# A spectral mixer with a gated token MLP: two pairs of the way back share a visit of TensorE

## The chip, the core and the metric

The kernel runs on one core of a Trainium2 chip. The metric is the device time of one execution in microseconds. Three runs of the kernel before took 365.48, 365.69 and 365.95 us; the median is 365.69 us.

## What is computed

x has 2048 tokens of 512 channels, all in fp32.

```python
xn = layernorm(x)                                   # over the channels
s  = irfft2(rfft2(xn) * (w_r + 1j * w_i))           # 2-D FFT over tokens and channels, filtered, and back
u  = gelu(einsum("bsd,sf->bdf", xn, w1) + b1)       # MLP over the tokens: 2048 -> 1792
y  = einsum("bdf,fs->bds", u, w2) + b2              # 1792 -> 2048
out = x + s * silu(transpose(y))
```

## The kernel before

The first 200 us or so make the layer norm, the way there of the transform, the filter, and the hidden layer `u`. The change touches only what follows: the second matrix product and the way back of the transform, in the loop over `p` (lines 1038 to 1099).

**Pairs and products.** The 2048 output tokens are 16 blocks of 128 rows. Blocks `p` and `p + 8` are a pair; there are eight. Each pair's output (2 blocks by 512 channels) is a 2 by 2 product of blocks, made with seven products in place of eight (a Strassen form). Their order is `ORDER = (1, 2, 5, 6, 3, 7, 4)`; the place of a product in it, 0 to 6, is called its slot `k`. A product is 21 matmuls of 128x128 weights by 256 columns (seven hidden tiles, each in three parts of a high and a low split), all into one half bank of PSUM. Products 1, 6, 7 and 4 go to `bx` (bank 3 for even pairs, bank 2 for odd ones), 2 to `by` (bank 4), 5 and 3 to `bz` (bank 5), each in the left half. Products 1, 2 and 5 start an accumulation; 6, 7, 4 and 3 add to what is there, so the state in between has to be read first: `p1`, `p5`, `v2` are copies by ScalarE, and `c11`, `c12`, `c22` are sums that VectorE reads out of PSUM. `c22 = bx + p5` is read after product 7 and before product 4.

**Forms.** The weights of a product are a "form" of w2: a high part that ScalarE makes (line 820) and a low part that VectorE makes (line 824), in three rotating buffers `w2f`. In slot `k` the form for the product three slots later is made, in the buffer that the product of slot `k` has just read. After product 7 VectorE also makes sums of blocks for the next pair (`sums_of_blocks`, two operations of 128x896). The w2 blocks come by DMA from SyncE; two sums of blocks per pair are made by a second, accumulating DMA from GpSimd, which waits for the first one to land.

**The way back.** For each pair, four gathers copy the pair's filtered rows out of `ey` into `yt` (two on ScalarE, then two on VectorE). TensorE then has three small parts, which are called a visit here: E (`even_channels`, 16 matmuls of a 64x64 quarter of the array, fp32, each recorded twice), O (`odd_channels`, four of 128x128), both from `yt` into banks 6 and 7, and S (`spectral`, four 64x64 matmuls by 512 columns, from `y` into banks 0 and 1). Between the channel parts (E, O) and the token part (S) stands `unfolded`, a generator of three pieces: a copy by ScalarE and five VectorE operations into `es`; a sum into `y`; a difference into `y`. `finish` multiplies S's result by the gate (`Silu`, ScalarE) into `r`, and four DMAs of GpSimd's queue add `r` to the output in memory, which holds x already; two of them belong to each block.

**Where it stands.** `SLOTS` gives for each pair the slot after which the visit stands, and a plan: after which slots a gather ("g") or a piece of `unfolded` ("s") is made. `PARTS` gives the order of E, S and O in the visit. In pair 0, E stands after slot 5 and O after slot 6; in pairs 1 to 6 the visit ESO stands after slot 5, with the S of the pair before; in pair 7 SEO after slot 3, and its own S after slot 5. So in pairs 0 to 7 something of the way back stands between products 7 and 4.

**What sets the order.** From line 937 on, every engine's instructions are kept in the order of the program (`Kept`), so each engine has one fixed queue. Waits come from the data: a tile's new use waits for the readers of its old one, and PSUM is followed by bank.

**Buffers.** The pool `fin` holds `es`, `y` and `yt` with one buffer each, `r` with two (one for each block of a pair), `c` with two and the gates `g` with four.

Of the kernel before, what the change touches and what calls it, by code (L numbers as in the profile page):

```python
# [9 lines left out]
F32 = mybir.dt.float32  # L10
F32R = mybir.dt.float32r
AF = mybir.ActivationFunctionType
# [3 lines left out]
P = 128  # L16
# [18 lines left out]
WT = 3  # L35


SLOTS = ((6, {3: "gggg", 6: "s"}), (5, {0: "s", 1: "sgg", 2: "gg", 5: "s", 6: "s"}),
         (5, {0: "s", 1: "gg", 2: "gg", 5: "s", 6: "s"}),
         (3, {0: "s", 1: "gg", 2: "gg", 3: "s", 4: "ss"}))  # L40

PARTS = ("O", *["ESO"] * 6, "SEO")

KD = np.concatenate([np.arange(0, 256, 4), np.arange(2, 256, 4), np.arange(1, 256, 2)])

# [94 lines left out]
def spectral_mixer_kernel(tc, x, w1, b1, w2, b2, wk, we, wx, c_f, c_ft, c_d, c_i, c_g, c_h, out):  # L142
# [19 lines left out]
    with tc.tile_pool(name="ps", bufs=1, space=PSUM) as psp, ExitStack() as left, ExitStack() as right:  # L162
# [778 lines left out]
        def new_sums(p):  # L941
            return (fp.tile([P, 2, 2, 2, P], F32, name=f"es{p}", tag="es"),
                    fp.tile([P, 2, 2, 2, P], F32, name=f"y{p}", tag="y"))

        def new_gates(p):
            return [fp.tile([P, D], F32, name=f"g{j}", tag="g", bufs=4) for j in (p, p + NP)]


        first_sums, gates = new_sums(0), {0: new_gates(0)}
# [3 lines left out]
        def gathered(p):  # L953


            yt = fp.tile([P, 2, 4, 2, 64], F32, name=f"yt{p}", tag="yt")
            yts[p] = yt
            for i, j in enumerate((p, p + NP)):
                for h in range(2):
                    to = yt[:, i, :, h ^ i].rearrange("p b (s c) -> p b s c", c=2)  # L960
                    yield V.tensor_copy(to, ey[:, :, h::2, j]) if i else A.activation(to, ey[:, :, h::2, j], AF.Copy)

        def tokens_of(yt, i, b):
            return yt[:, i, b].rearrange("p e c -> p (e c)")

        def even_channels(p):


            for i in range(2):
                for s in range(2):  # L970
                    at = slice(128 * i + 64 * s, 128 * i + 64 * s + 64)
                    for e in range(2):
                        for r, rows in enumerate((slice(0, 64), slice(64, P))):
                            T.matmul(ps[64 * e:64 * e + 64, 6 + r, at], yts[p][rows, i, 2 * s, e], ci[rows, 2 * s, :64],
                                     start=True, stop=True)

        def odd_channels(p):

            for i in range(2):
                for s in (1, 0):  # L980
                    at = 256 + 128 * s
                    T.matmul(ps[:, 6 + i, at:at + P], tokens_of(yts[p], i, 2 * s + 1), ci[:, 2 * s + 1], start=True, stop=True)

        def unfolded(p):

            es, y = new_sums(p) if p else first_sums
            e0, e1 = (es[:, :, k].rearrange("p i b c -> p i (b c)") for k in range(2))
            first, odd = ps[:, 6, :256].rearrange("p (i s c) -> p i s c", s=2, c=64), ps[:, 6:8, 256:]
            other = y.rearrange("p i h q c -> p (i h q c)")[:, :257]
            A.activation(other, ps[:, 7, :257], AF.Copy)  # L990
# [12 lines left out]
            ys[p] = y.rearrange("p i h q c -> p i (h q c)")  # L1003
            yield

        def spectral(p):

            y = ys.pop(p)
            for e, cols in enumerate((slice(0, 64), slice(64, P))):
                for r, rows in enumerate((slice(0, 64), slice(64, P))):  # L1010
                    i = e ^ r
                    T.matmul(ps[cols, i], cft[rows, cols], y[rows, i], start=True, stop=True)

        def gate(g, j, cols, src, scale):
            A.activation(g[:, cols], src, AF.Silu, bias=b2t[:, j:j + 1], scale=scale)
# [5 lines left out]

        def finish(g, j, cols):
            r = last_rows[:, j // NP] if last_rows is not None else fp.tile([P, D], F32, name=f"r{j}", tag="r", bufs=2)
            for to, a, b in zip(mirrored(r[:, cols], True), mirrored(ps[:, j // NP, cols], False), mirrored(g[:, cols], False)):
                V.tensor_mul(to, a, b)
            if last_rows is not None:
                for part in quarter_rows if cols is left_ else (cols,):
                    V.tensor_add(r[:, part], r[:, part], xr[j // NP][:, part])
            for queue, (rows, tokens) in zip((SY, SY if cols is right_ else A), halved):
                if last_rows is None:  # L1030
                    G.dma_start(out[tokens, j, cols], r[rows, cols], accum_op=ALU.add)
                else:
                    queue.dma_start(out[tokens, j, cols], r[rows, cols])
# [4 lines left out]
        for p in range(NP):  # L1038
            j0, j1 = p, p + NP
            more = p + 1 < NP  # L1040
            if p:
                gates[p] = new_gates(p)
            g0, g1 = gates[p]
            bx, by, bz = banks(p)
            slot, plan = SLOTS[min(p, 2) + (not more)]
            gathering = gathered(p)
            for k, n in enumerate(ORDER):
                started = not p and k < 2
                if not started:
                    products(p, n)  # L1050
                if n == 1 and p:
                    p1 = copied(f"p1_{p}", bx, w2p)
                elif n == 5:
                    p5 = copied(f"p5_{p}", bz, fp)
                elif n == 6:
                    v2 = copied(f"v2_{p}", bx, fp)
                elif n == 7:
                    c22 = summed(f"c22_{p}", bx, p5)
                if n == 3 and more:
                    c12 = summed(f"c12_{p}", bz, v2)  # L1060
                if not started:
                    ready.extend(w for w in [next(wforms, None)] if w is not None)
                if n == 2:
                    c11 = summed(f"c11_{p}", by, p1)
                elif n == 6:
                    gate(g0, j0, left_, c11, 1.0)
                elif n == 3 and more:
                    gate(g0, j0, right_, c12, 1.0)
                elif n == 7:
                    gate(g1, j1, right_, c22, -1.0)  # L1070
                elif n == 4:
                    for cols in (left_,) if more else quarter_rows:
                        gate(g1, j1, cols, bx[:, cols], -1.0)
                if not p and k == slot - 1:
                    even_channels(p)
                if k == slot:
                    for part in PARTS[p]:
                        {"S": spectral, "E": even_channels, "O": odd_channels}[part](p - (part == "S"))
                    yts.pop(p)
                    pieces = unfolded(p)  # L1080
                    if p:
                        for g, j in zip(gates.pop(p - 1), (j0 - 1, j1 - 1)):
                            finish(g, j, whole)
                for what in plan.get(k, ""):
                    next(gathering if what == "g" else pieces)
                if n == 3 and not more:
                    gate(g0, j0, right_, summed(f"c12_{p}", bz, v2), 1.0)
                if more and n == 7:
                    sums_of_blocks()
                if not more and k == 2:  # L1090
                    xr = [where.tile([P, NH * P], F32, name=f"xr{i}", tag="s1", bufs=1)[:, :D] for i, where in enumerate((w2p, fp))]
                    for to, j in zip(xr, (j0, j1)):
                        for rows, tokens in halved:
                            SY.dma_start(to[rows], x[tokens, j])
# [43 lines left out]
```

## Time and profile before

| | |
|---|---|
| median of three runs | 365.69 us |
| the profiled execution | 365.77 us |
| its span | 364.0 us |
| TensorE busy (share of the span) | 358.1 us (98%) |
| VectorE busy | 307.8 us (85%) |
| ScalarE busy | 211.2 us (58%) |
| GpSimd busy | 87.2 us (24%) |
| granted TensorE clock in the stage of the pairs | 1.00 |
| pair 2, 241.6 to 261.4 us: TensorE, VectorE, ScalarE busy | 19.80, 15.73, 10.66 us |

The span is the time from the first to the last instruction that the profiler recorded; the execution's own time is 1.77 us longer. In rows of the timeline the first number is the start in us from the span's start, the second the length of the row; rows of one kind that follow each other are merged, with their count at the end. The end of a matmul is modelled, so the start of the next row is the better measure of how long a group took. The bracket at the end of a row names idle time of the engine and what ended it. PE is TensorE, PEld its weight loads, DVE VectorE, ACT ScalarE, POOL GpSimd.

### The profile page before, as it was taken

What the parts mean: (1) busy time and instruction counts of PE and PEld (TensorE: products, weight loads), DVE (VectorE), ACT (ScalarE), POOL (GpSimd) and SP (SyncE); (2) the same over time, 40 slices, a digit from 0 to 9 for tenths busy, and PEclk for the clock granted to TensorE, in tenths of its full rate; (3) what the DMA queues carried; (4) which work ended last, traced back from release to release, by engine and by line L of the source; (5) the groups of instructions that cost most, each with busy time, mean ns of one, the idle gap of its engine ahead of it and who ended that gap; (6) DMA issues with size and microseconds to landing.
All of it is one profiled execution on the core that took longest, in us unless ns stands there. A gap on an engine that the chain in (4) does not pass through costs nothing.

```text
span 364.0 us, 8851 instructions
## 1 busy us (share of the span) xinstructions
PE 358.1 (98%) x3476; PEld 310.8 (85%) x3476; DVE 307.8 (85%) x590; ACT 211.2 (58%) x385; POOL 87.2 (24%) x134
## 2 busy tenths in 40 slices
PE   8999999999999999999999999999999999999994
PEld 7788888888877778777888999989898989898993
DVE  5899999967699997999995988687887878797974
ACT  4877778867634426755237884655464546565431
POOL 4233333323222012220120001040503132130330
PEclk9999999999999999999999999999999999999999
DMA  7977999306695687996577288698888989898624
GB/s 207 246 190 187 231 288 333 133 0 155 172 275 181 189 241 193 252 239 201 174 236 156 101 236 172 180 185 200 189 184 212 178 224 164 240 162 209 114 27 90
DMA packets 33293, 68.66 MB, mean 189 GB/s; under 512 B 4612, under 2 KB 19380, under 8 KB 33124
## 3 DMA queue, kind: packets, MB, share of 16 engines
q1 hardware_dynamic: 24276, 42.44, 42.2%
q0 software_dynamic: 8496, 25.01, 32.0%
q10 hardware_dynamic: 480, 0.66, 0.6%
q8 instruction: 27, 0.44, 0.6%
q14 instruction: 14, 0.11, 0.1%
HBM read 59.70 MB, written 8.13 MB: 186 GB/s over the span
## 4 chain that ended last, share of the span: by engine, by line
PE 96%; DVE 1%; DMA 1%; issue 0%; ACT 0%; DVEq 0%
PE ps L139 96%; DMA x<-in_x_dram 1%; DVE stm L244 0%; DVE rows L139 0%; DVE h L469 0%; DVE w1l L469 0%; DVE h L272 0%; ACT g L139 0%; DVE v2m L221 0%; DVE mvm L220 0%; DVE tm L229 0%; ACT sdm L223 0%; DVEq L1134 0%; DVE r0m L228 0%; DVE nbm L237 0%
## 5 line engine op out<-in xcount | busy, mean ns | idle before, releaser
L139 PE MATMUL ps<-h,w1h 128*128 128x512 f32 x400 | 116.3, 397 | 0.1
L139 PEld LDWEIGHTS ps<-h,w1h 128*128 128x128 f32 x400 | 72.9, 188 | 19.9 <-issue 4.9
L139 PE MATMUL ps<-h,w1l 128*128 128x512 f32 x200 | 67.6, 390 | 0.0
L139 DVE TENSOR_TENSOR w2f<-a,w2f 128x896 fp32r<-128x896 f32 x36 | 39.2, 1090 | 16.4 <-ACT w2f L139 16.4
L139 ACT ACTIVATE w2f<-a 128x896 fp32r<-128x896 f32 x36 | 37.2, 1033 | 20.0 <-PE ps L139 7.6
L139 PEld LDWEIGHTS ps<-h,w1l 128*128 128x128 f32 x200 | 37.5, 188 | 8.1
L139 PE MATMUL ps<-fb,w2f 128*128 128x256 f32 x336 | 42.1, 280 | 0.0
L139 POOL DMA_DIRECT2D s<-in_w_dram x14 | 18.3, 1311 | 96.8 <-DMA s<-in_w_dram 71.7
L139 PE MATMUL ps<-fa,w2f 128*128 128x256 f32 x336 | 41.4, 278 | 0.0
L139 PEld LDWEIGHTS ps<-fb,w2f 128*128 128x128 f32 x336 | 39.9, 188 | 0.9 <-DVE c L139 0.8
L139 PE MATMUL ps<-fc,w2f 128*128 128x256 f32 x336 | 39.9, 277 | 0.0
L139 PEld LDWEIGHTS ps<-fa,w2f 128*128 128x128 f32 x336 | 39.9, 188 | 0.0
L139 PEld LDWEIGHTS ps<-fc,w2f 128*128 128x128 f32 x336 | 39.2, 188 | 0.0
L155 ACT ACTIVATE w1h<-w1s 128x512 fp32r<-128x512 f32 x26 | 16.2, 632 | 25.6 <-PE ps L139 10.8
L139 POOL DMA_DIRECT2D out_dram<-r x28 | 23.6, 1276 | 27.9 <-DVE r L139 27.9
L667 POOL DMA_DIRECT2D xc<-xc x16 | 9.8, 619 | 69.2 <-ACT xc L665 54.0
L308 POOL TENSOR_TENSOR ey<-t 128x256 f32<-128x256 f32 x16 | 15.7, 979 | 44.0 <-DVE t L306 44.0
L139 ACT ACTIVATE w2f<-s 128x896 fp32r<-128x896 f32 x15 | 15.3, 1022 | 14.2 <-PE ps L139 12.4
L139 DVE TENSOR_TENSOR w2f<-s,w2f 128x896 fp32r<-128x896 f32 x15 | 16.3, 1088 | 6.5 <-ACT w2f L139 6.4
L469 DVE TENSOR_TENSOR w1l<-w1r,w1h 128x384 fp32r<-128x384 f32 x32 | 21.3, 669 | 0.0
L139 PE MATMUL ps<-fd,w2f 128*128 128x256 f32 x168 | 20.7, 278 | 0.0
L268 ACT ACTIVATE h<-x,nbm,rsm 128x256 f32<-128x256 f32 (+1 forms) x34 | 18.4, 593 | 3.9 <-DVE nbm L263 3.1
(132 smaller groups left out, 602.3 us busy)
## 6 DMA issues: line engine op xcount, KB each, us to landing
a<-in_w_dram SPq DMA_DIRECT2D x22, 448.0 KB, 4.0
wt<-in_wk_dram POOLq DMA_DIRECT2D x16, 512.0 KB, 5.8
s<-in_w_dram SPq DMA_DIRECT2D x16, 448.0 KB, 4.1
s<-in_w_dram POOLq DMA_DIRECT2D x16, 448.0 KB, 6.5
w1s<-in_w_dram SPq DMA_DIRECT2D x52, 128.0 KB, 5.5
w1r<-in_w_dram SPq DMA_DIRECT2D x28, 192.0 KB, 5.1
xc<-xc POOLq DMA_DIRECT2D x16, 256.0 KB, 3.1
out_dram<-in_x_dram SPq DMA_DIRECT2D x4, 960.0 KB, 6.5
```

Source lines behind the costliest of these rows:

```text
L139: return lambda *args, **kw: self.keep(operation(*args, **kw))
L155: return A.activation(hi, src, AF.Copy), V.tensor_sub(lo, src, hi.bitcast(F32))
L268: keep(A.activation(to, v, AF.Identity, bias=m["nb"][:, i], scale=m["rs"][:, i, 1:2]))
L308: G.tensor_add(ey[:, 0::3, :, j], a, b)
L469: keep(V.tensor_sub(dst, src, hi.bitcast(F32)))
L667: keep(G.dma_start(*(v.rearrange("p s t c -> p s (t c)") for v in (there[c::2], here[1 - c::2, ::-1]))))
```

## The change

- Pair 0 has no visit; its gathers stay after slot 3. They go to two tiles of tag `r`, and so do those of pair 2.
- Pair 1's visit stands after slot 3 and holds E of pairs 0 and 1 and O of pairs 0 and 1. Pair 1's go to banks 0 and 1 (`transformed_to`). The gathers of pair 1 stand one slot earlier, after slots 0 and 1. `unfolded` of pair 0 stands after slots 3 and 4, that of pair 1 after slots 5, 6 and slot 0 of pair 2.
- Pair 2's visit stands after slot 4 and holds E of pair 2, S of pairs 0 and 1, and O of pair 2. S of pair 0 goes to bank 2 and, in two halves, to the right halves of banks 4 and 5 (`spectral_places`): six matmuls instead of four. `finish` of pair 0 stands after slot 4, with four multiplies of 128x128 in place of two of 128x256 for its second block; that of pair 1 after slot 5.
- `unfolded` of pair 2 stands after slot 6 and slot 0 of pair 3. From pair 3's visit on, all is as before.
- Tiles of the first pairs take other places: pair 0's `y` and pair 2's `es` that of `yt`, one gate of pair 2 that of `es`.

The diff, without changes of form alone:

```diff
-SLOTS = ((6, {3: "gggg", 6: "s"}), (5, {0: "s", 1: "sgg", 2: "gg", 5: "s", 6: "s"}),
-         (5, {0: "s", 1: "gg", 2: "gg", 5: "s", 6: "s"}),
-         (3, {0: "s", 1: "gg", 2: "gg", 3: "s", 4: "ss"}))
-PARTS = ("O", *["ESO"] * 6, "SEO")
+SLOTS = ((7, {3: "gggg"}), (3, {0: "gg", 1: "gg", 3: "s", 4: "ss", 5: "s", 6: "s"}),
+         (4, {0: "s", 1: "gg", 2: "gg", 6: "s"}), (5, {0: "ss", 1: "gg", 2: "gg", 5: "s", 6: "s"}),
+         (5, {0: "s", 1: "gg", 2: "gg", 5: "s", 6: "s"}), (3, {0: "s", 1: "gg", 2: "gg", 3: "s", 4: "ss"}))
...
+        def new_gate(j):
+            return fp.tile([P, D], F32, name=f"g{j}", tag="g", bufs=4)
+
         def new_gates(p):
-            return [fp.tile([P, D], F32, name=f"g{j}", tag="g", bufs=4) for j in (p, p + NP)]
+            if p == 2:
+                return [fp.tile([P, 2, D], F32, name="g2", tag="es")[:, 0], None]
+            return [new_gate(j) for j in (p, p + NP)]
...
-            yt = fp.tile([P, 2, 4, 2, 64], F32, name=f"yt{p}", tag="yt")
+            if p in (0, 2):
+                yt = [fp.tile([P, D], F32, name=f"yt{p}_{i}", tag="r", bufs=2) for i in range(2)]
+                yt = [t.rearrange("p (b h c) -> p b h c", b=4, h=2) for t in yt]
+            else:
+                yt = fp.tile([P, 2, 4, 2, 64], F32, name=f"yt{p}", tag="yt")
+                yt = [yt[:, i] for i in range(2)]
...
+        def transformed_to(p):
+            return 0 if p == 1 else 6
...
+        def unfolded_to(p):
+            if p > 2:
+                return new_sums(p)
+            es = first_sums[0] if p == 0 else fp.tile([P, 2, 2, 2, P], F32, name=f"es{p}", tag=("es", "yt")[p - 1])
+            y = first_sums[1] if p == 1 else fp.tile([P, 2, 2, 2, P], F32, name=f"y{p}", tag=("yt", "y")[p // 2])
+            return es, y
...
+        def spectral_places(p):
+            if p:
+                return [[(whole, ps[:, i])] for i in range(2)]
+            return [(whole, ps[:, 2])], [(left_, ps[:, 4, HD:]), (right_, ps[:, 5, HD:])]
+
         def spectral(p):
-            y = ys.pop(p)
+            y, places = ys.pop(p), spectral_places(p)
             for e, cols in enumerate((slice(0, 64), slice(64, P))):
                 for r, rows in enumerate((slice(0, 64), slice(64, P))):
                     i = e ^ r
-                    T.matmul(ps[cols, i], cft[rows, cols], y[rows, i], start=True, stop=True)
+                    for part, to in places[i]:
+                        T.matmul(to[cols], cft[rows, cols], y[rows, i, part], start=True, stop=True)
...
-            for to, a, b in zip(mirrored(r[:, cols], True), mirrored(ps[:, j // NP, cols], False), mirrored(g[:, cols], False)):
-                V.tensor_mul(to, a, b)
+            for part, src in spectral_places(j % NP)[j // NP] if cols is whole else [(cols, ps[:, j // NP, cols])]:
+                for to, a, b in zip(mirrored(r[:, part], True), mirrored(src, False), mirrored(g[:, part], False)):
+                    V.tensor_mul(to, a, b)
...
-            slot, plan = SLOTS[min(p, 2) + (not more)]
+            slot, plan = SLOTS[min(p, 4) + (not more)]
...
-                if not p and k == slot - 1:
-                    even_channels(p)
                 if k == slot:
-                    for part in PARTS[p]:
-                        {"S": spectral, "E": even_channels, "O": odd_channels}[part](p - (part == "S"))
-                    yts.pop(p)
-                    pieces = unfolded(p)
-                    if p:
-                        for g, j in zip(gates.pop(p - 1), (j0 - 1, j1 - 1)):
+                    done = (0, 1) if p == 1 else (p,)
+                    back = (0, 1) if p == 2 else (p - 1,) if p > 2 else ()
+                    for at in done[:1] if back else done:
+                        even_channels(at)
+                    for at in back:
+                        spectral(at)
+                    for at in done:
+                        odd_channels(at)
+                        yts.pop(at)
+                    pieces = chain(*map(unfolded, done))
+                    if back:
+                        for g, j in zip(gates.pop(back[0]), (back[0], back[0] + NP)):
                             finish(g, j, whole)
+                if p == 2 and k == slot + 1:
+                    for g, j in zip(gates.pop(1), (1, 1 + NP)):
+                        finish(g, j, whole)
```

More of the change, by code (lines that the diff above doesn't have):

```diff
@@ L959, in gathered @@
                 for h in range(2):
-                    to = yt[:, i, :, h ^ i].rearrange("p b (s c) -> p b s c", c=2)
+                    to = yt[i][:, :, h ^ i].rearrange("p b (s c) -> p b s c", c=2)
                     yield V.tensor_copy(to, ey[:, :, h::2, j]) if i else A.activation(to, ey[:, :, h::2, j], AF.Copy)
         def tokens_of(yt, i, b):
-            return yt[:, i, b].rearrange("p e c -> p (e c)")
+            return yt[i][:, b].rearrange("p e c -> p (e c)")
+        def transformed_to(p):
+            return 0 if p == 1 else 6
         def even_channels(p):
+            bank = transformed_to(p)
             for i in range(2):
@@ L973, in even_channels @@
                         for r, rows in enumerate((slice(0, 64), slice(64, P))):
-                            T.matmul(ps[64 * e:64 * e + 64, 6 + r, at], yts[p][rows, i, 2 * s, e], ci[rows, 2 * s, :64],
+                            T.matmul(ps[64 * e:64 * e + 64, bank + r, at], yts[p][i][rows, 2 * s, e], ci[rows, 2 * s, :64],
                                      start=True, stop=True)
@@ L981, in odd_channels @@
                     at = 256 + 128 * s
-                    T.matmul(ps[:, 6 + i, at:at + P], tokens_of(yts[p], i, 2 * s + 1), ci[:, 2 * s + 1], start=True, stop=True)
+                    T.matmul(ps[:, transformed_to(p) + i, at:at + P], tokens_of(yts[p], i, 2 * s + 1), ci[:, 2 * s + 1], start=True, stop=True)
+        def unfolded_to(p):
[4 more added lines that the diff above has]
+            return es, y
         def unfolded(p):
-            es, y = new_sums(p) if p else first_sums
+            es, y = unfolded_to(p)
+            bank = transformed_to(p)
             e0, e1 = (es[:, :, k].rearrange("p i b c -> p i (b c)") for k in range(2))
-            first, odd = ps[:, 6, :256].rearrange("p (i s c) -> p i s c", s=2, c=64), ps[:, 6:8, 256:]
+            first, odd = ps[:, bank, :256].rearrange("p (i s c) -> p i s c", s=2, c=64), ps[:, bank:bank + 2, 256:]
             other = y.rearrange("p i h q c -> p (i h q c)")[:, :257]
-            A.activation(other, ps[:, 7, :257], AF.Copy)
+            A.activation(other, ps[:, bank + 1, :257], AF.Copy)
             other = other[:, :256].rearrange("p (i s c) -> p i s c", s=2, c=64)
@@ L1069, in spectral_mixer_kernel @@
                 elif n == 7:
+                    if g1 is None:
+                        g1 = gates[p][1] = new_gate(j1)
                     gate(g1, j1, right_, c22, -1.0)
```

## The prediction

> **What bounds the kernel now.** I read the page first, then TensorE's timeline of the last stage, the waits, and the timelines of VectorE, ScalarE and GpSimd around one visit.
>
> ```profile
> span 364.0 us, 8851 instructions
> ...
> PE 96%; DVE 1%; DMA 1%; issue 0%; ACT 0%; DVEq 0%
> ```
>
> The profiled execution took 365.77 us, 1.77 more than its span; the median of the runs shown is 365.69. The chain that ended last is TensorE for 96% of the span, so in the last stage whatever lengthens TensorE's stream lengthens the kernel. That stream is, for each pair, seven products of 21 matmuls (numbers 1, 2, 5, 6, 3, 7, 4, in slots 0 to 6) and a visit of the way back: E (even channels), O (odd channels), S (token transform). Pair 0 first, then pair 1:
>
> ```profile
> 212.65 2.64 PE L139 MATMUL ps<-fa,w2f 128*128 128x256 f32 x21
> 215.13 2.63 PE L139 MATMUL ps<-fb,w2f 128*128 128x256 f32 x21
> 217.69 0.69 PE L139 MATMUL ps<-cd,yt 64*64 64x64 f32 x32
> 218.31 2.74 PE L139 MATMUL ps<-fb,w2f 128*128 128x256 f32 x21
> 220.89 1.05 PE L139 MATMUL ps<-cd,yt 128*128 128x128 f32 x8
> 221.70 2.72 PE L139 MATMUL ps<-fd,w2f 128*128 128x256 f32 x21
> ```
>
> ```profile
> 234.15 2.63 PE L139 MATMUL ps<-fb,w2f 128*128 128x256 f32 x21
> 236.72 0.69 PE L139 MATMUL ps<-cd,yt 64*64 64x64 f32 x32
> 237.23 1.04 PE L139 MATMUL ps<-y,cft 64*64 64x512 f32 x8
> 238.20 1.16 PE L139 MATMUL ps<-cd,yt 128*128 128x128 f32 x8
> 239.12 2.72 PE L139 MATMUL ps<-fb,w2f 128*128 128x256 f32 x21
> ```
>
> A product takes 2.47 us from start to start (212.65 to 215.13). A visit costs its own rows, 0.10 at its entry (234.15 + 2.47 = 236.62, E at 236.72) and 0.09 in the product behind it (2.72 against 2.63). In pair 1 E takes 0.51, S 0.97 and O 0.92.
>
> **What the visits hide.** Products 7 and 4 stand next to each other and add into the same bank; between them VectorE must read the bank (`c22`). Everywhere else a whole product lies between a product and the one that adds to its result.
>
> ```profile
> PEld ps L139 <- DVE c L139: 0.8, 1, 0.8
> ```
>
> ```profile
> 217.80 0.42 DVE L139 TENSOR_TENSOR c<-ps,p 128x256 f32<-128x256 f32 x1
> ```
>
> Pair 0 shows the wait: product 7 ends at 217.76 (215.13 + 2.63), `c22` runs from 217.80 to 218.22, product 4 starts at 218.31, 0.09 later. Without the wait it would start at 217.60, so the wait is 0.71; E ran under it for nothing. Product 4 then takes 0.11 more than usual (218.31 to 220.89 is 2.58). From pair 1 on the whole visit covers it. The change moves the visits of pairs 0, 1 and 2 away from this gap.
>
> **The change, part by part** (against 365.77).
>
> (1) Pair 0 has no visit. E lay under the wait, which stays: 0. O goes: 0.81 (220.89 to 221.70) + 0.09 in the product behind it: **-0.90**.
>
> (2) Pair 1's visit, now in slot 3, loses S (0.97) and holds E and O of two pairs: 0.51 more for E, 0.81 more for an O behind an O (as in pair 0, where it also stood behind matmuls of its own shape), and one change of shape from E to O that I take as 0.10, by the entry: **+0.45**. The gathers move one slot ahead, onto VectorE and ScalarE time that is free there; their cost is 0, and at most their 0.5 us on a queue.
>
> (3) In pair 1, product 4 now waits for `c22` openly, and `c22` comes late, because VectorE has the unfolding of pair 0 before it:
>
> ```profile
> 256.71 0.42 DVE L139 TENSOR_TENSOR c<-ps,p 128x256 f32<-128x256 f32 x1 [0.29 <-PE ps L139]
> 257.85 1.09 DVE L139 TENSOR_TENSOR w2f<-a,w2f 128x896 fp32r<-128x896 f32 x1 [0.71 <-ACT w2f L139]
> 258.86 1.41 DVE L139 TENSOR_TENSOR r<-ps,g 128x256 f32<-128x256 f32 x4
> 260.19 0.61 DVE L139 TENSOR_TENSOR es<-ps,y 128x256 f32<-128x256 f32 x2
> ...
> 262.43 1.08 DVE L139 TENSOR_TENSOR a<-a,s 128x896 f32<-128x896 f32 x1
> 263.55 1.09 DVE L139 TENSOR_TENSOR a<-a,a 128x896 f32<-128x896 f32 x1
> 264.55 1.08 DVE L139 TENSOR_TENSOR w2f<-s,w2f 128x896 fp32r<-128x896 f32 x1
> 265.56 0.69 DVE L139 TENSOR_TENSOR y<-es 128x512 f32<-128x512 f32 x1
> 266.16 1.09 DVE L139 TENSOR_TENSOR w2f<-a,w2f 128x896 fp32r<-128x896 f32 x1
> ```
>
> ```profile
> 256.76 1.05 ACT L139 ACTIVATE w2f<-a 128x896 fp32r<-128x896 f32 x1 [1.06 <-issue]
> 257.71 0.50 ACT L139 ACTIVATE g<-c,b2t 128x256 f32<-128x256 f32 x1
> 259.29 0.39 ACT L139 ACTIVATE y<-ps 128x257 f32<-128x257 f32 x1 [1.08 <-PE ps L139]
> ```
>
> ```profile
> 254.04 2.63 PE L139 MATMUL ps<-fb,w2f 128*128 128x256 f32 x21
> ...
> 259.01 2.63 PE L139 MATMUL ps<-fb,w2f 128*128 128x256 f32 x21
> 261.47 2.54 PE L139 MATMUL ps<-fd,w2f 128*128 128x256 f32 x21
> ...
> 340.81 2.54 PE L139 MATMUL ps<-fa,w2f 128*128 128x256 f32 x21
> ```
>
> Let T be the first matmul behind the visit (259.01 in these rows). ScalarE's copy ends at T + 0.67 (259.29 + 0.39); the five `es` operations take 2.24 (260.19 to 262.43) and end at T + 2.9. Product 3 ends at T + 2.72. Then, in VectorE's fixed order: `c12` to T + 3.3; the low part of the next form, which starts 1.18 after its product's end (254.04 + 2.63 = 256.67, low part at 257.85), T + 3.9 to 4.9; the two `y` operations at 0.6 each (265.56 to 266.16) to 6.1; `c22` to 6.53; product 4 at T + 6.62. Without a wait it would start at T + 5.03 (2 x 2.47 + 0.09). The wait is 1.59, and 0.11 for the start after it: **+1.70**. Bounds: 0.71, if `c22` finds VectorE free as in pair 0, and 2.0, if the low part comes 0.3 later.
>
> (4) Pair 2's visit, in slot 4, holds E, two S and O: a second S is 0.97. The first S has its second signal in halves, in banks 4 and 5, so six matmuls in place of four. No row shows two quarter-array matmuls of one quadrant in line beside whole ones. If the four quadrants still run side by side it costs nothing; if each half waits for the one before it, S grows by about 0.9, a second S; fully in line 1.7. I take 0.9, since the issue order puts the halves of one quadrant one behind the other: **+1.87** (0.97 to 2.6).
>
> (5) Pair 2's gap between 7 and 4 is open too, with VectorE free by then: 0.71 + 0.11 = **+0.82**.
>
> (6) Two finishes now stand one slot apart, but `r` has two buffers. `finish` of pair 1 must wait until the DMAs of pair 0's `r` have landed; queued behind it on VectorE are the sums of blocks and then the low part of the form for pair 3's third product, for which TensorE waits.
>
> ```profile
> 259.90 3.37 POOL L139 DMA_DIRECT2D out_dram<-r  x4 [2.84 <-DVE r L139]
> 262.11 2.09 POOL L139 DMA_DIRECT2D s<-in_w_dram  x1
> ```
>
> ```profile
> DMA to landing us min/median/max: 3.1/4.7/5.6
> ```
>
> ```profile
> L139 DVE TENSOR_TENSOR rows<-ps,g 128x128 f32<-128x128 f32 x4 | 1.0, 287 | 0.6 <-ACT g L139 0.6
> ```
>
> With T behind pair 2's visit: `r` lies where the gathered tokens lay, so `finish` of pair 0 starts when O has ended, T + 0.3; GpSimd issues 1.04 later (258.86 to 259.90), four issues 0.55 apart, the last at T + 3.0; by the median it lands at T + 7.7. (The four quarter-width multiplies, 287 ns each, are done by T + 2.1, in time for the third issue.) The second half of pair 1's finish runs to 8.5, the sums of blocks (2.12, 262.43 to 264.55) to 10.6, the low part to 11.65. TensorE would want it at T + 10.8: product 4 at 3.27, then 2.58 and two of 2.47. Wait: 0.95. Behind that low part stand the five `es` operations of pair 2 (2.24) and the next low part (1.0): 3.25 for a slot of 2.47, 0.78 more. Together **+1.7**; bounds 0 (landing in 3.1) and 3.3 (5.6, which pushes the low part 0.9 later, and 0.7 if pair 3's gather on ScalarE, which waits for the last `es` read, holds up a copy).
>
> By the Trainium skill, "SBUF — State Buffer", section "The DMA setup-cost knee", a transfer takes about 2 us and its bytes at 436 GB/s; for 128 KB that is an estimate of 2.3 us, and by it term (6) would be 0 and the sum 1.7 lower. The median of 4.7 in these rows speaks against it.
>
> By the Trainium skill, "TensorE: Matmul & The Clock Gate", section "Architectural detail: the array is 16× 32×32, not 1× 128×128", the queue can pull weight loads ahead of matmuls in flight; by it the 0.11 after each wait would fall away, 0.22 less in the sum. The wait row above is one of the weight load itself, so I keep it.
>
> **Sum:** -0.90 + 0.45 + 1.70 + 1.87 + 0.82 + 1.70 = +5.6. 365.77 + 5.6 = 371.4; less the 0.08 by which the profiled execution is above the median, **371.3 us**.
>
> **The rivals.**
>
> (A) The DMAs land early (3.1): the last at T + 6.1, finish to 6.9, low part by 10.1, before 10.8. Term (6) is 0: 369.6. The minimum is one of 15 issues, the median speaks against it; but the second DMA of a pair may find a quieter queue.
>
> (B) The pitch of the products. Rows of one form have two lengths: 2.63 up to 254.04, 2.54 from 261.47 to 340.81, 0.09 apart; the switch came at pair 2's visit, and nothing in the trace says why. If the changed visit doesn't bring it, the 28 products of pairs 3 to 6 and five around them keep the slow pitch: 33 x 0.09 = +3.0, 374.3.
>
> (C) The other side. The same pitch turns fast at the first open wait, in pair 0: product 4 of pair 0, seven of pair 1 and six of pair 2 gain 0.09 each, -1.3. That decides only where the added waits are small: with the lower bounds of all terms (-0.90 + 0.45 + 0.71 + 0.97 + 0.71 + 0) the sum is +1.94, and with the pitch +0.6, 366.3. For it: the state does change at such places. Against: pair 0's wait did not change it in the rows above.
>
> (D) The change doesn't open the gaps: something else still lies between `c22` and product 4, and the finishes don't wait. Then (3), (5) and (6) are 0 and +1.42 remains: 367.1. The order is pinned on every engine, so little speaks for this.
>
> **How the numbers follow.** Forecast 0.55, A 0.20, B 0.10, C 0.08, D 0.07. A difference below about 0.2%, 0.7 us, can't be told from none. C is half of it within and partly faster; several small terms at once give a little more to faster: faster 0.05, same 0.06, slower 0.89. The range takes A, B and D in and leaves most of C out: 367.0 to 374.4.
>
> **What would show it.** Right: no E or O rows in pair 0; in pairs 1 and 2 a weight load that waits on `c`, about 1.6 and 0.7; the long visits at 2.85 and 4.3 us; a wait of VectorE `r` on a DMA of `out_dram`, and a TensorE wait on `w2f` in pair 3. Wrong: `c22` read while TensorE goes on, an S in halves as short as one S, or products at 2.54 before pair 2.

## The result, and the profile after

The changed kernel takes 370.48 us (median of four, 370.26 to 371.13) against 365.82 us for the kernel before beside it (365.48 to 365.97): a ratio of 1.0132, 95% interval 1.0114 to 1.0149. Two later groups gave medians of 372.89 and 371.41 us against 365.67 and 365.69; over all 13 executions the changed kernel lies between 370.26 and 373.75 with a median of 371.38. The forecast was 371.3 (367.0 to 374.4).

The profiled execution took 371.13 us. Its page has, for the span and the chain that ended last:

```profile
span 369.4 us, 8860 instructions
...
PE 90%; DVE 4%; DMA 2%; issue 1%; ACT 1%; POOL 0%; DVEq 0%; ACTq 0%
```

The span grew by 5.4 us (364.0 before). TensorE still ends last, but 6% of the chain has gone from it to others: VectorE has 4% and DMA 2%, where both had 1%, ScalarE and issue 1% each, where both had 0%. TensorE's timeline shows where that is (start, length, and in brackets the idle time and what ended it):

```profile
215.32 2.63 PE L136 MATMUL ps<-fb,w2f 128*128 128x256 f32 x21
218.56 2.71 PE L136 MATMUL ps<-fb,w2f 128*128 128x256 f32 x21 [0.61 <-DVE c L136]
221.11 2.64 PE L136 MATMUL ps<-fd,w2f 128*128 128x256 f32 x21
...
231.09 3.14 PE L136 MATMUL ps<-cd,yt 64*64 64x64 f32 x80
233.99 2.72 PE L136 MATMUL ps<-fa,w2f 128*128 128x256 f32 x21
236.55 2.63 PE L136 MATMUL ps<-fb,w2f 128*128 128x256 f32 x21
240.64 2.71 PE L136 MATMUL ps<-fb,w2f 128*128 128x256 f32 x21 [1.46 <-DVE c L136]
243.19 2.63 PE L136 MATMUL ps<-fd,w2f 128*128 128x256 f32 x21
...
255.65 0.69 PE L136 MATMUL ps<-cd,yt 64*64 64x64 f32 x32
256.17 2.02 PE L136 MATMUL ps<-y,cft 64*64 64x512 f32 x20
258.12 1.16 PE L136 MATMUL ps<-cd,yt 128*128 128x128 f32 x8
259.03 2.72 PE L136 MATMUL ps<-fb,w2f 128*128 128x256 f32 x21
262.36 2.71 PE L136 MATMUL ps<-fb,w2f 128*128 128x256 f32 x21 [0.61 <-DVE c L136]
264.91 2.63 PE L136 MATMUL ps<-fd,w2f 128*128 128x256 f32 x21
...
269.86 5.11 PE L136 MATMUL ps<-fc,w2f 128*128 128x256 f32 x42
275.74 2.75 PE L136 MATMUL ps<-fa,w2f 128*128 128x256 f32 x21 [0.77 <-ACT p L136]
278.33 2.63 PE L136 MATMUL ps<-fb,w2f 128*128 128x256 f32 x21
...
283.29 2.63 PE L136 MATMUL ps<-fb,w2f 128*128 128x256 f32 x21
285.76 2.54 PE L136 MATMUL ps<-fd,w2f 128*128 128x256 f32 x21
...
353.09 0.46 PE L136 MATMUL ps<-cd,yt 64*64 64x64 f32 x16
353.72 0.46 PE L136 MATMUL ps<-cd,yt 64*64 64x64 f32 x16 [0.17 <-DVE yt L136]
...
355.88 2.72 PE L136 MATMUL ps<-fa,w2f 128*128 128x256 f32 x21
```

The matmul columns are all there; what is new is idle time between them. Four brackets that the kernel before did not have in these places: `c` in pair 0 (there E filled it), `c` in pairs 1 and 2, `p` in pair 3; and a small one in pair 7. From the first matmul of a pair to that of the next:

| stretch | before | after | difference | what it is |
|---|---|---|---|---|
| up to pair 0 | 202.76 | 202.96 | +0.20 | start of the stage, not from the change (202.67 and 202.80 in two later profiles of the changed kernel) |
| pair 0 | 18.94 | 18.15 | -0.79 | O gone |
| pair 1 | 19.98 | 22.08 | +2.10 | visit +0.50, wait 1.62, restart 0.08, O's exit of pair 0 gone -0.09 |
| pair 2 | 19.79 | 21.72 | +1.93 | visit +0.98, wait 0.77, restart 0.08, product 4 at the long pitch 0.09 |
| pair 3 | 19.24 | 20.85 | +1.61 | wait 0.94, restart 0.12, six products at the long pitch 0.56 |
| pairs 4 to 6 | 57.72 | 57.72 | 0 | |
| pair 7 up to the product behind its visit | 12.01 | 12.40 | +0.39 | visit E, S, O in place of S, E, O |
| rest | | | -0.07 | |

A wait here is the distance of the starts less the product's 2.47: in pair 1, 240.64 - 236.55 - 2.47 = 1.62. In pair 2 product 7 stands right behind the visit and takes 2.56 for itself: 262.36 - 259.03 - 2.56 = 0.77. The restart is what the product behind a wait takes beyond 2.47. The pitch is the distance between the starts of a product's matmuls, the two lengths of rival B. The sum is +5.37.

Pair 7 was not in the forecast. The list of parts `PARTS`, whose last entry "SEO" gave pair 7 its own order, is gone in the diff; the new loops make E, S, O for every pair from 2 on. (The description of the change above says that from pair 3's visit on all is as before; that is not so for pair 7.) In the kernel before, the same place reads:

```profile
348.05 1.09 PE L139 MATMUL ps<-y,cft 64*64 64x512 f32 x8
348.96 1.73 PE L139 MATMUL ps<-cd,yt 64*64 64x64 f32 x40
350.44 2.72 PE L139 MATMUL ps<-fa,w2f 128*128 128x256 f32 x21
```

S stood first and gave VectorE's gather its time: 2.39 from 348.05 to 350.44. After, E stands first, waits for `yt` between its halves (353.09 to 353.72), and the visit takes 2.79.

### The profile page after: what moved, and what is told of

It reads as the page before. It is cut to its first block, busy times and chain, and to the rows that moved or that the text cites. A ratio compares the mean times of both kernels' runs of the same rounds, so it can differ in the third digit from the quotient of the medians.

```text
span 369.4 us, 8860 instructions
## 1 busy us (share of the span) xinstructions
PE 359.4 (97%) x3480; PEld 311.8 (84%) x3480; DVE 308.0 (83%) x592; ACT 211.1 (57%) x385; POOL 87.3 (24%) x134
## 4 chain that ended last, share of the span: by engine, by line
PE 90%; DVE 4%; DMA 2%; issue 1%; ACT 1%; POOL 0%; DVEq 0%; ACTq 0%
PE ps L136 90%; DMA out_dram<-r 1%; DVE w2f L136 1%; DMA x<-in_x_dram 1%; DVE y L136 1%; DVE a L136 1%; ACT w2f L136 1%; DVE es L136 0%; POOL out_dram L136 0%; DVE r L136 0%; DVE c L136 0%; DVE rows L136 0%; DVE stm L241 0%; DVE yt L136 0%; DVE h L269 0%
## 5 line engine op out<-in xcount | busy, mean ns | idle before, releaser
L136 POOL DMA_DIRECT2D s<-in_w_dram x14 | 16.6, 1182 | 103.7 <-DMA s<-in_w_dram 69.0
```

Source lines behind the costliest of these rows:

```text
L136: return lambda *args, **kw: self.keep(operation(*args, **kw))
```

## The experiments

All of them compute the whole result. "Wait" and "visit" are read as above. Since the pitch of the products turned out to differ between executions of one kernel, each profiled execution is also brought to one pitch: a product at the short pitch (rows of 2.54, starts 2.38 apart) is 0.093 us shorter than one at the long pitch (2.63, 2.47 apart), so 0.093 for each short one is added to the span.

| kernel | median us (lowest to highest, n) | profiled span | short products of 56 | span with all at the long pitch |
|---|---|---|---|---|
| before | 365.7 or 365.8 in each group | 364.0 | 33 | 367.1 |
| changed | 370.48 (370.26 to 371.13, 4) | 369.4 | 26 | 371.8 |
| after2 | 372.89 (371.30 to 373.75, 5) | 371.1 | 6 | 371.7 |
| after3 | 371.41 (371.12 to 373.18, 4) | 369.6 | 24 | 371.8 |
| a_seo | 370.96 (370.76 to 373.04, 5) | 369.0 | 26 | 371.4 |
| a_r3 | 370.02 (369.76 to 370.11, 4) | 368.2 | 26 | 370.6 |
| a_r3seo | 369.77 (369.62 to 370.15, 4) | 367.9 | 24 | 370.1 |
| a_late | 373.07 (370.52 to 374.90, 6) | 368.7 | 35 | 372.0 |
| a_cov | 367.91 (366.52 to 369.06, 6) | 367.3 | 2 | 367.5 |
| b_p1s4 | 367.14 (366.75 to 367.95, 5) | 365.4 | 34 | 368.6 |
| b_split | 369.29 (369.18 to 369.50, 4) | 367.4 | 0 | 367.4 |
| b_e6 | 366.62 (366.39 to 369.81, 12) | 368.0 | 2 | 368.2 |
| b_seo | 366.79 (366.67 to 366.98, 6) | 365.0 | 23 | 367.1 |

The changed kernel's three spans, 369.4, 371.1 and 369.6, become 371.8, 371.7 and 371.8. At one pitch the change costs 4.7 us; the rest of what is measured is pitch.

**The gap between products 7 and 4, alone (b_p1s4).** The kernel before with pair 1's visit one slot earlier.

```diff
-SLOTS = ((6, {3: "gggg", 6: "s"}), (5, {0: "s", 1: "sgg", 2: "gg", 5: "s", 6: "s"}),
+SLOTS = ((6, {3: "gggg", 6: "s"}), (4, {0: "s", 1: "sgg", 2: "gg", 5: "s", 6: "s"}),
```

> The kernel before, with nothing moved but pair 1's visit, from slot 5 to slot 4, so that nothing stands between products 7 and 4 of pair 1. Theory (open gap): TensorE waits 0.77 us for c22 there and its next product is 0.1 us longer: 365.8 + 0.85 = 366.6, with a wait of that size on c in pair 1's rows. Rival (the price of the changed kernel is in the long visits and the merged work, the gap is hidden by the queue of weight loads): 365.8, no wait on c.

Measured 367.14 us, +1.5. TensorE's timeline of this kernel:

```profile
219.01 2.75 PE L139 MATMUL ps<-fb,w2f 128*128 128x256 f32 x21 [0.57 <-DVE c L139]
...
237.34 2.63 PE L139 MATMUL ps<-fb,w2f 128*128 128x256 f32 x21
240.58 2.71 PE L139 MATMUL ps<-fb,w2f 128*128 128x256 f32 x21 [0.61 <-DVE c L139]
```

Pair 1 has the wait of pair 0 now: 240.58 - 237.34 - 2.47 = 0.77. That is the gap's price where VectorE is free, and the rival, no wait on `c`, is refuted. Pair 0's own wait, which the edit does not touch, was 0.65 longer in this execution (1.36 against 0.71): a w2 block landed at 216.36 (215.46 before), and the low part of the form made from it stood ahead of `c22` on VectorE. The two together, 0.77 + 0.08 + 0.65, are the 1.5 of the profiled execution (367.22). In the other profiles that show its landing it lands by 215.5, so the second part looks like one load's landing and not like the edit; whether the four executions without a profile had it too is not shown.

**c22 late behind VectorE (a_late).** The changed kernel with the two `y` pieces of pair 0 behind `c22` of pair 1.

```diff
-SLOTS = ((7, {3: "gggg"}), (3, {0: "gg", 1: "gg", 3: "s", 4: "ss", 5: "s", 6: "s"}),
+SLOTS = ((7, {3: "gggg"}), (3, {0: "gg", 1: "gg", 3: "s", 5: "sss", 6: "s"}),
```

> The changed kernel with the two later pieces of pair 0's unfolding (two VectorE operations of 0.6 us) moved behind the read c22 of pair 1. Theory: c22 finds VectorE free, the wait between products 7 and 4 of pair 1 falls from 1.5-1.6 us to the 0.77 us of pairs 0 and 2: about 369.7 against 370.5. The work behind c22 is the same in sum, so nothing is given back unless pair 2's forms come late (then up to 0.6). Rival: c22 is late because of the low part of the form before it, not because of the two pieces: 370.3 or more.

In this kernel's timeline of TensorE:

```profile
238.99 2.71 PE L136 MATMUL ps<-fb,w2f 128*128 128x256 f32 x21 [0.61 <-DVE c L136]
...
267.92 4.49 PE L136 MATMUL ps<-fc,w2f 128*128 128x256 f32 x35
272.85 1.06 PE L136 MATMUL ps<-fc,w2f 128*128 128x256 f32 x7 [0.44 <-DVE w2f L136]
275.11 2.74 PE L136 MATMUL ps<-fa,w2f 128*128 128x256 f32 x21 [1.20 <-ACT p L136]
```

VectorE's waits for the DMAs of `r` in it (total, times, longest):

```profile
DVE r L136 <- DMA out_dram<-r: 2.7, 2, 2.1
```

The wait in pair 1 fell from 1.62 to 0.77, so the two `y` operations were its late part. But the 369.7 of the theory did not come: in pair 3 the wait on `p` grew and one on `w2f` came, behind waits of `r` on its DMAs of 2.7 in place of 1.6. The four DMAs of pair 0's `r` took 5.4 to 5.7 us to land in this execution, where the changed kernel's took 3.3 to 4.7; whether the edit did that is not shown, so the run shows what part of pair 1's wait was the queue, and not what the edit is worth. At one pitch the span is 0.2 above the changed kernel's. The median, 373.07 (2.6 above it), was not taken apart: only the quickest execution, 370.52, has a profile, and from 370.5 to 374.9 is more than all 35 short products (3.3) explain.

**The place of r (a_r3).** The changed kernel with a third place for one block's `r`, the unused half of the tile that pair 2's gate lies in.

```diff
-                return [fp.tile([P, 2, D], F32, name="g2", tag="es")[:, 0], None]
+                both = fp.tile([P, 2, D], F32, name="g2", tag="es")
+                spare.append(both[:, 1])
+                return [both[:, 0], None]
...
-            r = last_rows[:, j // NP] if last_rows is not None else fp.tile([P, D], F32, name=f"r{j}", tag="r", bufs=2)
+            r = last_rows[:, j // NP] if last_rows is not None else spare.pop() if j == 1 else fp.tile([P, D], F32, name=f"r{j}", tag="r", bufs=2)
```

> The changed kernel with a free place for pair 1's r of block 1 (the unused half of the tile that holds a gate of pair 2), so that the two finishes in a row have three places for r instead of two. Theory: VectorE's waits of 0.33 and 1.31 us on the landing DMAs go, everything behind them on VectorE moves ahead by about 1.6 us, ScalarE's gather of pair 3 (which waited 3.5 us for VectorE's last read of es) starts 1.6 us earlier, and the 0.94 us that TensorE waited in pair 3 for the copy behind that gather, with the 0.1 us of its start, go: about 369.4 against 370.5. Rival: the backlog is VectorE's own work (two finishes, the unfolding and the sums in three slots), and TensorE waits in pair 3 nearly as long: 370.2 or more.

TensorE in pair 3 of this kernel:

```profile
269.70 5.11 PE L136 MATMUL ps<-fc,w2f 128*128 128x256 f32 x42
274.65 2.63 PE L136 MATMUL ps<-fa,w2f 128*128 128x256 f32 x21
```

```profile
DVE r L136 <- DMA out_dram<-r: 0.5, 1, 0.5
```

The wait on `p` is gone (274.65 against 275.74), the waits on `c` are as they were, and the time is 370.02: 1.2 less at one pitch. Of VectorE's 1.6 of waiting for the DMAs of `r`, 0.5 is left, and it no longer matters: the copy `p` ends at 274.30, before product 3 starts. So it is the two places of `r` that made pair 3's wait; the rival, VectorE's own work, is refuted.

**The order in pair 7 (a_seo), and both (a_r3seo).** S before E in pair 7, without and with the third place.

```diff
+                    if not more:
+                        spectral(p - 1)
                     for at in done[:1] if back else done:
                         even_channels(at)
-                    for at in back:
+                    for at in back if more else ():
                         spectral(at)
```

> The changed kernel with pair 7's visit again in the order S, E, O (the change had turned it into E, S, O along with the others). Theory: in the changed kernel E of pair 7 waits 0.38 us for VectorE's gather, which S would cover; with S first the 0.4 us come back: about 370.1 against 370.5, pair 7's visit from its first matmul to the next product 2.4 us instead of 2.79, no weight load that waits on the gather. Rival: the gather is late for itself and O, behind E, waits as long: no change.

> The changed kernel with both edits of before: the third place for the result r of block 1 and the order S, E, O in pair 7. Theory (the wait of pair 3 and the order of pair 7 are separate terms that add): against the changed kernel of the same group at the same pitch of the products, pair 3 about 1.0 shorter and pair 7 0.40 shorter, together 1.4 lower; the visits of pairs 1 and 2 and the waits on c (0.77, 1.60, 0.77) stay, so it is still about 3.5 to 4 above the kernel before. Rival (the time lost in pair 3 comes back in a later pair, or the pitch decides): less than 0.7 lower, or a difference that goes with the pitch of rows (2.63 against 2.54) and not with the two edits.

Pair 7's visit takes 2.40 again (353.09 to 355.49 in a_seo, 351.98 to 354.38 in a_r3seo), and the spans at one pitch fall by 0.3 and, with the third place, by 1.7. The medians do not show the 0.3 of a_seo (370.96 against 370.48 in the other group); it lies within what the pitch does from group to group. Both terms add.

**The changed kernel again (after2, after3).**

> The changed kernel itself once more, beside the other kernels of this group. Theory: 370.3 to 371.1 as before, with the same waits: 0.77 on c in pairs 0 and 2, 1.5 to 1.6 in pair 1, about 0.9 on the copy p in pair 3; the products' pitch may switch at another visit than pair 3's, worth up to 0.65 us either way.

> The changed kernel unchanged, as the measure for the other in this group. If the two lengths of a product's row (2.63 and 2.54) are what sets its times apart, they lie between 370.3 and 373.8 in groups, and the profiled execution's excess over 364.0 is 5.4 plus 0.093 for each product that is slow where it was fast before; if they are not, the excess can't be had from that count.

The waits are the same in all three profiles (0.61, about 1.45 and 0.61 in the brackets on `c`; 0.77, 1.06 and 0.99 on `p`). What differs is the pitch, and by more than the 0.65 that was allowed for it: after2 was forecast at 370.3 to 371.1 and took 372.89. In its profile the pitch stayed long behind pair 3's visit,

```profile
285.37 2.64 PE L136 MATMUL ps<-fd,w2f 128*128 128x256 f32 x21
```

where the first profile has 285.76 with 2.54. after3's excess over 364.0 is 5.6, and by the count 5.4 + 2 x 0.093 = 5.6.

**S in halves (b_split).** The kernel before with the second signal of S in two halves, in every pair.

```diff
-                    T.matmul(ps[cols, i], cft[rows, cols], y[rows, i], start=True, stop=True)
+                    for part in (left_, right_) if i else (whole,):
+                        T.matmul(ps[cols, i, part], cft[rows, cols], y[rows, i, part], start=True, stop=True)
```

> The kernel before, with the second signal of S in halves in every pair (six matmuls in place of four, same bank). The term I gave 0.9 us in the sum. Theory after the changed kernel's trace (two S, one of them in halves, took 1.95 us, twice 0.97): halves cost nothing, 365.7, each S still 0.97 to 1.0 to the next matmul. Rival (the first reckoning): 0.9 us for each of eight S, 372.

The rows of S and of O behind it, in pair 1:

```profile
237.29 1.09 PE L139 MATMUL ps<-y,cft 64*64 64x512 f32 x12
238.31 1.16 PE L139 MATMUL ps<-cd,yt 128*128 128x128 f32 x8
```

S takes 1.02 in place of 0.97: halves cost 0.05 in each of the six visits E, S, O and 0.01 or 0.02 in pair 7, and at one pitch the span is 0.4 above the kernel before. The rival's 0.9 for each S is refuted. The median is 3.6 higher all the same; in the profiled execution no product had the short pitch, 33 x 0.093 = 3.1, which with the 0.4 makes the 3.5 between the two spans.

**E in the open (b_e6).** The kernel before with pair 0's E moved out of the gap, to O in front of pair 1.

```diff
-PARTS = ("O", *["ESO"] * 6, "SEO")
+PARTS = ("EO", *["ESO"] * 6, "SEO")
...
-                if not p and k == slot - 1:
-                    even_channels(p)
```

> The kernel before, with E of pair 0 moved from the gap between products 7 and 4 to just before O. Theory (E ran under the wait for c22 and cost nothing there): the wait stays at about 0.7 to 0.8, and E now costs its 0.5 and a change of shape of 0.2: 366.3 against 365.7, pair 0 longer by 0.6. Rival (a visit costs its own time wherever it stands): 365.7, pair 0 no longer than before.

```profile
215.24 2.63 PE L139 MATMUL ps<-fb,w2f 128*128 128x256 f32 x21
218.48 2.71 PE L139 MATMUL ps<-fb,w2f 128*128 128x256 f32 x21 [0.61 <-DVE c L139]
```

Pair 0's wait on `c` stays (0.77 by the starts, 0.71 with E under it) and pair 0 grows by 0.85, so E had been free under the wait. Twelve executions fall on two levels: eight from 366.39 to 366.62 and four from 369.43 to 369.81. The distance, 3.1, is again 33 x 0.093, and the profiled execution, one of the four, has two short products. The eight have no profile: that they had 33 more is read from the distance alone.

**S first in every visit (b_seo).**

```diff
-PARTS = ("O", *["ESO"] * 6, "SEO")
+PARTS = ("O", *["SEO"] * 7)
```

> The kernel before with S, E, O instead of E, S, O in the visits of pairs 1 to 6: the same parts and as many changes of shape. By the lengths of the visits 0 (pair 7 has this order before the change and its visit is 2.39 against 2.40). Theory (the state of the pitch is set anew at each interruption of the stream, by its timing, not by the parts in it): the times fall on one of a few levels, 365.7 if the pitch turns fast at pair 2's visit, up to 3.1 higher if it stays slow, up to 1.3 lower if it turns fast before it. Rival (the pitch follows the phase of the run, by time, not the interruptions): within 0.3 of 365.7, with the switch near 259 us.

At one pitch it is the kernel before (367.1), as its visits say. The rival, a switch near 259 us by time alone, did not come: the pitch changed at every visit of pairs 1 to 6. The second product behind the visits of pairs 1, 2 and 3:

```profile
241.49 2.54 PE L139 MATMUL ps<-fd,w2f 128*128 128x256 f32 x21
...
260.82 2.63 PE L139 MATMUL ps<-fd,w2f 128*128 128x256 f32 x21
...
280.62 2.54 PE L139 MATMUL ps<-fd,w2f 128*128 128x256 f32 x21
```

23 short products where before has 33: 10 x 0.093 = 0.9 of the 1.1 in the medians.

**Merged visits that cover the gap (a_cov).** All that was learned put together: the merged visits back in slot 5, E of pair 0 in its gap, the third place of `r`, the pieces of `unfolded` spread so that none stands ahead of a `c22`, S first in pair 7.

```diff
...
+SLOTS = ((7, {3: "gggg"}), (5, {0: "gg", 1: "gg", 5: "s", 6: "ss"}),
+         (5, {0: "s", 1: "sgg", 2: "sgg"}), (5, {0: "s", 1: "s", 2: "s", 3: "gg", 4: "gg", 5: "s", 6: "s"}),
          (5, {0: "s", 1: "gg", 2: "gg", 5: "s", 6: "s"}), (3, {0: "s", 1: "gg", 2: "gg", 3: "s", 4: "ss"}))
...
+                if not p and k == 5:
+                    even_channels(0)
...
```

> The changed kernel with its merged visits moved back over the gap between products 7 and 4: E of pair 0 there in pair 0, and after slot 5 E of pair 1 with both O in pair 1, and E, both S and O in pair 2; the pieces of the unfolding spread over the next slots, a third place for r, pair 7 in the order S, E, O. Theory (the loss is the open gaps, the two places of r and pair 7's order, and merging itself is worth a tenth or two): no wait on c beyond pair 0's 0.2 to 0.9, none in pair 3; 365.4 to 366.2, the same as before. Rival (long visits and merged work cost by themselves): 368 or more.

367.91 us, where the theory said 365.4 to 366.2 and the rival 368 or more. Pair 1's gap is covered:

```profile
235.96 2.68 PE L136 MATMUL ps<-cd,yt 64*64 64x64 f32 x48
238.39 2.72 PE L136 MATMUL ps<-fb,w2f 128*128 128x256 f32 x21
```

No wait on `p` or `w2f` is left, and at one pitch it is 4.3 below the changed kernel but still 0.4 above the kernel before. What lies beyond that is pitch: the profiled execution (369.06) has two short products where before has 33, 2.9 us. Its quickest executions, 366.5, are above 365.7 too. Merging visits in itself brought nothing measurable; no version beat the kernel before.

## Why the prediction was right, point by point

**Term 1 (pair 0, -0.90)**: right. -0.79 in pair 0 and -0.09 in the product behind O, -0.88. That E had been free is shown by b_e6.

**Term 2 (pair 1's visit, +0.45)**: +0.50 (2.90 against 2.40).

**Term 3 (pair 1's open gap, +1.70)**: right step by step, 1.62 + 0.08. VectorE in pair 1, with T = 233.99:

```profile
234.74 0.62 DVE L136 TENSOR_TENSOR es<-ps,y 128x256 f32<-128x256 f32 x2 [1.13 <-ACT y L136]
...
235.66 1.41 DVE L136 TENSOR_TENSOR es<-es,ps 128x512 f32<-128x512 f32 x2
...
237.86 1.09 DVE L136 TENSOR_TENSOR w2f<-a,w2f 128x896 fp32r<-128x896 f32 x1 [0.46 <-ACT w2f L136]
238.87 1.29 DVE L136 TENSOR_TENSOR y<-es 128x512 f32<-128x512 f32 x2
240.07 0.42 DVE L136 TENSOR_TENSOR c<-ps,p 128x256 f32<-128x256 f32 x1
```

Low part at T + 3.87 (forecast 3.9), the `y` operations to 6.08 (6.1), `c22` to 6.50 (6.53), product 4 at 6.65 (6.62). The a_late run shows which part of it was the queue (0.85) and b_p1s4 which the bare gap (0.77).

**Term 4 (pair 2's visit, +1.87)**: mis-sized, +0.98 measured. The step that failed is the 0.9 for S in halves, which stood on the issue order alone; S in halves cost 0.05 in b_split, and two S of 20 recorded matmuls took 1.95 here (256.17 to 258.12), twice 0.97, and 1.88 in a_cov. The bound from below, 0.97, was the value.

**Term 5 (pair 2's gap, +0.82)**: +0.85 (0.77 and 0.08). The restarts after the waits measured 0.08, 0.08 and 0.12, for a forecast of 0.11 each. By the Trainium skill, "TensorE: Matmul & The Clock Gate", section "Architectural detail: the array is 16× 32×32, not 1× 128×128", the queue can pull weight loads ahead; in these rows that did not take the restart away.

**Term 6 (two places of r, +1.70)**: +1.06, and by another path. The DMA part held: forecast to land at T + 7.7, second half of the finish to 8.5 and the low part to 11.65, with T = 259.03 now. VectorE of the changed kernel:

```profile
264.30 0.76 DVE L136 TENSOR_TENSOR r<-ps,g 128x256 f32<-128x256 f32 x2 [0.33 <-DMA out_dram<-r]
266.37 0.76 DVE L136 TENSOR_TENSOR r<-ps,g 128x256 f32<-128x256 f32 x2 [1.31 <-DMA out_dram<-r]
```

The four took 3.3, 3.7, 4.2 and 4.7 us from issue to landing, the last to 266.25 (T + 7.2); the finish ended at T + 8.1 and the low part at T + 11.2. The estimate of 2.3 us by the Trainium skill, "SBUF — State Buffer", section "The DMA setup-cost knee", is not borne out by these four. What failed is the sentence that TensorE wants that low part at T + 10.8. That is when the product starts, but its 21 matmuls use the high part in the first 14 and the low part in the last 7; so it was wanted 14/21 x 2.47 = 1.65 later. The rows x35 and x7 in a_late show it: the wait on `w2f` falls after 21 + 14 matmuls. With that, the forecast's own 11.65 would have been in time (10.8 + 1.65 = 12.45), and so would the next low part; that 1.70 came near 1.06 is luck. (The forecast's working is also 0.1 off: 11.65 - 10.8 is 0.85, which makes 0.95 only with a restart of 0.1.) What was late instead is ScalarE:

```profile
274.66 0.75 ACT L136 ACTIVATE yt<-ey 128x256 f32<-128x256 f32 x2 [3.54 <-DVE y L136]
275.32 0.37 ACT L136 ACTIVATE p<-ps 128x256 f32<-128x256 f32 x1
```

Pair 3's gather goes into the place where pair 2's `es` lies, so it waits until VectorE's last read of `es` is done; VectorE is late by the 1.64 it waited for `r` (0.33 + 1.31). Behind the gather in ScalarE's queue stands the copy `p`, which must read product 5's bank before product 3 adds to it. This path was in the forecast only as 0.7 in the upper bound. a_r3 shows that the cause is `r`: with a third place VectorE is on time, but for 0.5, and TensorE's wait is gone.

**Missing**: pair 7's order, +0.39. It could be read in the diff, and the forecast put it at nothing.

**The rivals.** A (the DMAs land early) and D (no gaps) did not come: the waits are there in all three profiles of the changed kernel. B (the pitch does not turn where it did) came in part in the first profile, for seven products (0.65), and in full in after2, where all 33 kept the long pitch (3.1) and six others had the short one. C's event, a short pitch from pair 0's wait on, came too, in after2 and after3, for five products, but it did not last beyond pair 1's visit. Of the signs, the long visits were 2.90 and 3.38 (forecast 2.85 and 4.3), and the TensorE wait on `w2f` in pair 3 did not come: it was one on `p`. Two of the signs of being wrong came: an S in halves as short as one S, which is term 4, and in after2 and after3 products at 2.54 before pair 2. The forecast's sum was for one pitch: +5.6 against 4.7 measured there. Term 4 too high by 0.89 and term 6 by 0.64 were offset by 0.39 in pair 7, by 0.2 ahead of the stage and, in the total, by the pitch (0.65). The time was right partly because errors cancelled.

## What to carry to other kernels

When an insertion stands between a producer and a consumer, ask first what its time covers: moving two visits out of the gap between products 7 and 4 cost a wait of 0.77 where VectorE was free and 1.62 where its queue held other work ahead of the read. Follow a late buffer through every engine's fixed queue, and note at which instruction of the consumer it is really needed; the wait showed on ScalarE's copy, two dependencies away from the DMA. Read the diff for what it deletes too, and, where equal instructions have two lengths in the profile, count them before comparing times.

## What the runs showed of the hardware

The same 128x256 matmuls, at a granted clock of 1.00, run at one of two pitches, 113.3 or 117.8 ns from start to start. The table of windows of the kernel before (the granted clock is the third figure from the end of a row) for a stretch at the long pitch and one at the short:

```profile
241.70:256.00 14.30, 14.30 (x124) 14.30 (x123) 11.34 (x16) 8.82 (x14) 2.67 (x4) 1.00 0.84 171
...
261.50:275.00 13.50, 13.50 (x122) 13.50 (x121) 10.98 (x16) 8.79 (x14) 2.71 (x4) 1.00 0.85 178
```

Clock, DMA share and the other engines' work are alike in both. The visits do not follow the pitch: from E to the next product it is 2.40 us in pair 1 (236.72 to 239.12) and also in pair 3, between products of the short pitch (275.85 to 278.25), where a clock 4% higher would have made it 2.31. In all 13 profiles the pitch changes only where TensorE's stream is interrupted, at a visit or at a wait, and never within an unbroken run of products. Which pitch follows an interruption is not fixed by the kernel's code: behind pair 3's visit the changed kernel had the short one in its first profile and the long one in after2. Nor is it the chip alone: the executions of b_e6, all on one chip, fall on two levels 3.1 us apart. The kernel before lay between 365.03 and 366.24 in all its executions, within 1.2 us. Bringing spans to one pitch leaves the three profiles of the changed kernel 0.1 apart where they were 1.7 apart. What decides it is open; a distance of 200 or 201 ns between the first two matmuls behind an interruption went with the short pitch in before and in the first profile at 283.29, but in after2 also with the long one at 282.81, so that is no rule.

Two 64x64 matmuls of half the columns, one behind the other in a quarter of the array beside whole ones in the others, cost at most 0.05 us per S more than whole ones (b_split, both halves into one bank). In the changed kernel, with the halves in two banks, two S of which one had halves took 1.95, and 1.88 in a_cov, against 1.94 for twice a whole one.
